# Four real rows as one group of 64-row halves, and planned steps moved behind a section's last tile

## The chip, the cores and the metric

The kernel runs on one core of a Trainium2 chip. The metric is the device time of one execution in microseconds (us). TensorE (PE) multiplies, VectorE (DVE) takes maxima and evacuates, ScalarE (ACT) does exponentials and copies, GpSimd (POOL) does elementwise work, SyncE (SP) issues most DMAs.

## The reference

Two token mixers read the same x (2048 x 512), and a gate per token blends them:

```python
g = sigmoid((x * gate_w).sum(-1))
# A: DFT along the hidden axis, then along the sequence, real part
a = x @ dft_hid_re.T;  b = x @ dft_hid_im.T
A = dft_seq_re @ a - dft_seq_im @ b
# B: attention, 32 heads of 16
q, k, v = split(x @ wqkv)
B = (softmax(q @ k.T * 16**-0.5) @ v) @ wo
out = g * A + (1 - g) * B
```

All arrays are float32. The kernel keeps the accuracy by splitting operands in a high and a low part and adding three products (high with high, high with low, low with high).

## The kernel before

**Units and streams.** Heads go in 16 pairs; head h of a pair (h is 0 or 1) has its stacked q and k in partitions 64h to 64h+49 of the tiles qs and ks (two buffers, by the pair's parity). A *unit* is one pair, one half of the queries (hf, 1024 of them) and one block of 128 keys; there are 512, 32 to a pair. Two kinds of PE tile are made of qs and ks, each 128 x 512 and of 64 rows of PE:

- an *s tile* (scores(), L720) is a block of scores; ACT takes its exponential into pt (L721). There are 2 x 512 for each half h.
- an *a tile* (a_tile(), L222) is a block of scores of which DVE takes the row maxima (L224). The a stream runs 48 a half ahead of the s stream (LEAD); when 64 a tiles of a pair's query half are done, m_parts() and m_rows() put the negated maxima as two extra rows into qs (4 DMAs on SP, 4 on POOL), which the s tiles of that half need.

values() takes two units' pt and does their value products (pv(), L756, 128 rows x 32 columns, four side by side); ACT copies the sum to oe (L765), POOL adds it to osum (L771) in add_sums().

**Sections.** PE's order is written by hand. A tile uses only 64 of PE's 128 rows, so in a *section* (segment()) the products of the Fourier part run in one half of the rows while tiles of the other half's stream run beside them; two sections in a row take the same products in half 0 and then in half 1, into one bank (d_bank, psD), which completes the sum. The strings FULL (16 slots), THIN (14) and NINE give a section's tiles: "s" and "a" have a product beside them, "aS" and "sA" are a tile of each half with no product, and "|" ends it with values(). pairs() yields 13 pairs of THIN sections (12 products, one row block of the real part each), 96 pairs of FULL (16 products of the sequence DFT) and 13 of NINE (9 products of the output projection).

**Ahead of the sections**, four() makes row blocks in groups of four chains: each phase runs two chains side by side, one in each half of the rows, and the halves are swapped in the later phases; after products 3 and 8 of a phase maxima() issues a pair of a tiles. Chain groups of v and of the imaginary part b are made so. The first three row blocks of the real part (real(), L416, then real_next(): ACT copies the bank to y, two buffers, and POOL splits y into the two halves of ab[s]) are done in 128-row products, six at a time (pump()), with four tiles after each six and one values() among them.

**Behind the sections** a loop over the last ten pairs of units issues eight s tiles, some whole products of the projection (table whole) and one values() each, and last_pair() ends the kernel.

**The plan.** at(u, f, ...) notes a step for unit u, and run_plan(u) runs what is noted up to u + 1. Steps are load_stacks() (12 DMAs on SP that load a pair's qs and ks), sums() and inverse() (the softmax sums' reciprocals), block() (normalising a block of outputs: loads on SP, a multiply on POOL, then a cast on ACT, a subtraction on POOL and a DMA), load_yg() and last_block(). deferred holds m_parts and m_rows, of which each section's end runs one.

**Banks.** bank() takes of seven PSUM banks the one that a small model (now, free, dve, act) expects to come free first. Every engine works through its own instructions in the order written.

Of the kernel before, what the change touches and what calls it, by code (L numbers as in the profile page):

```python
# [9 lines left out]
F32 = mybir.dt.float32  # L10
# [5 lines left out]
P = 128  # L16
S = 2048
D = 512
# [4 lines left out]
NT = S // P  # L23
# [8 lines left out]
def mix_kernel(ctx: ExitStack, tc: tile.TileContext, xa_t, xa, wqkv, w_hid, w_seq, wo, gate_w, out):  # L32
# [264 lines left out]
    def maxima():  # L297

        nonlocal a_next
        users = [a_tile(a_next, h) for h in range(2)]  # L300
        a_next += 1
        return users[1]

    def four(ss, wh, wl, done):

        ps = [turn_of("s") for _ in ss]
        seen = None
        for phase, pair in enumerate(((0, 1), (2, 3), (1, 0), (3, 2))):
            guard, seen = seen, None
            both = [row_products(ss[c], wh, wl) for c in pair]  # L310
            for j in range(12):
                for half, c in enumerate(pair):
                    st, mv = next(both[half])
                    r = slice(64 * half, 64 * half + 64)
                    i = nc.tensor.matmul(ps[c], st[r], mv[r], start=phase < 2 and j == 0, stop=phase > 1 and j == 11)  # L315
                    if phase > 1 and j == 0:
                        tc.add_manual_dep(
                            i.ins, guard.ins.name,
                            mybir.DependencyInfo(mybir.DependencyClass.Sync, mybir.DependencyReason.DATA))
                if j in (3, 8):  # L320
                    user = maxima()
                    seen = seen or user
            if deferred:
                deferred.pop(0)()
            if phase > 1:
                for c in sorted(pair):
                    done(ss[c], ps[c])
# [10 lines left out]
    def spare(i, dt, name):  # L338

        return const.tile([P, 4, P], dt, name=name, tag=f"w{i}")  # L340
# [40 lines left out]
    def bank(i=None):  # L381

        nonlocal now
        if i is None:
            i = min(range(7), key=lambda j: free[j])
        now = max(now, free[i] + 0.7)
        return i, banks[i].tile([P, 512], F32, name="t")

    def read_by(i, kind):

        nonlocal dve, act
        if kind == "a":
            dve = max(now + 2.0, dve) + 2.6
            free[i] = dve + 0.4
        else:
            act = max(now + 2.0, act) + 2.1
            free[i] = act + 0.5
# [21 lines left out]

    def real():  # L420

        for s, t in enumerate(ab):
            chain = Chain(d_bank, 12)
            for kt in range(KT):
                h1, l1 = (t[:, v, kt * P:(kt + 1) * P] for v in range(2))
                yield chain, h1, wre[0][kt], None
                yield chain, h1, wre[1][kt], None
                yield chain, l1, wre[0][kt], partial(real_next, s, t, chain) if kt == KT - 1 else None
# [186 lines left out]
    def load_yg(hf, ts):  # L615
        for t in ts:
            if hf:
                yp[t] = spare(t - 8, F32, f"yp{t}").rearrange("p a b -> p (a b)")
            elif t < 3:
                yp[t] = work.tile([P, D], F32, name=f"yp{t}", tag="y" if t else "yr", bufs=2 if t else 1)  # L620
        if not hf and ts[-1] == 7:
            for x, n in (("qs0", 4), ("ks0", 1)):
                y4 = main.tile([P, n, D], F32, name=f"yp_{x}", tag=x)
                yp.update({(3 if n == 4 else 7) + j: y4[:, j] for j in range(n)})
        for t in ts:
            nc.sync.dma_start(yp[t], yg_d[t])

# [76 lines left out]

    pts = {}

    def scores(u, qb, h):
        p, r = divmod(u, 32)
        hf, kt = divmod(r, 16)
        q0 = hf * 1024 + qb * 512  # L710
        if u >= UNITS - 16:

            blk, kt = divmod(kt, 8)
            q0, kt = 1024 + blk * 512, 2 * kt + qb
        if u not in pts:
            pts[u] = work.tile([P, 4, 512], F32, name="pt", bufs=4)
        i, ps = bank()
        read_by(i, "s")
        rr = slice(64 * h, 64 * h + 50)
        nc.tensor.matmul(ps, ks[p % 2][rr, kt * P:(kt + 1) * P], qs[p % 2][rr, q0:q0 + 512], start=True, stop=True)  # L720
        return nc.scalar.activation(pts[u][:, 2 * qb + h], ps, AF.Exp, bias=0.0, scale=DH ** -0.5)  # L721
# [54 lines left out]
    def add_sums():  # L776
        while adds:
            adds.pop(0)()
# [26 lines left out]
    def pump(gen, n):  # L805
        for x in take(gen, n, False):
            issue(x, None)
# [8 lines left out]
    def at(u, f, *args):  # L816
        plan.setdefault(u, []).append(partial(f, *args))
# [10 lines left out]
                        at(last + du + 8 * half, block, step, hf, ct, half)  # L828

    for p in range(1, NP):  # L830
        at(32 * (p - 1), load_stacks, p)
    one, more = [d_bank], [d_bank, o_bank, o_bank]
    at(456, load_yg, 0, range(3))
    at(481, load_yg, 0, range(3, 8))
    for step, u in enumerate((486, 490, 494)):
        at(u, last_block, step, 1, 3, nc.gpsimd)
    for step, u in enumerate((500, 506, 506)):
# [4 lines left out]
    def run_plan(u):  # L842
        for v in sorted(v for v in plan if v <= u + 1):
            for f in plan.pop(v):
                f()
# [31 lines left out]
    def values():  # L877
        nonlocal valued
        us = valued, valued + 1
        valued += 2  # L880
        add_sums()
        if us[0] < UNITS - 16:
            pv(us)
        else:
            for u in us:
                pv_last(u)

    def segment(pattern, half, ds, stop):


        nonlocal now
        nonlocal users
        before, users = users, []
        ds, late = iter(ds), []
        for slot in pattern.split():
            if slot == "|":
                for f in late:
                    f()
                values()
                continue  # L900
            now += 1
            if len(slot) == 1:
                x = next(ds, None)
                if x:

                    before = before if x[0].begun else None
                    i = issue(x, half, stop, late)
                    users = []
                    if before:
                        tc.add_manual_dep(  # L910
                            i.ins, dict(before).get("s", before[0][1]).ins.name,
                            mybir.DependencyInfo(mybir.DependencyClass.Sync, mybir.DependencyReason.DATA))
                        before = None
            score(slot[0], 1 - half)
            if len(slot) == 2:
                score(slot[1].lower(), half)
        if deferred:
            deferred.pop(0)()

    def pairs():  # L920

        for i in range(NT - 3):
            yield (THIN,) * 2, take(hid, 12)
        for i in range(2 * NT * 3):
            yield (FULL,) * 2, take(seq, 16)
        for gen, n in ((proj(1, (0, 1, 2), one), 8), (first, 5)):
            for i in range(n):
                yield NINE, take(gen, 9)

    first = proj(0, (0, 1, 2), one)  # L930
    run_plan(0)
    gate()
    hid, seq = real(), dft()
    for i in range(6):
        pump(hid, 6)
        if i < 4:
            for kind in "sa":
                for h in range(2):
                    score(kind, h)
        else:  # L940
            if i == 4:
                values()
            for _ in range(2):
                score("s", 0)
                score("a", 0)
    users = []
    for patterns, ds in pairs():
        for half in range(2):
            run_plan(valued)
            segment(patterns[half], half, ds, half == 1)  # L950


    run_plan(valued)
    for i in range(4):
        score("s", 1)
    run_deferred()
    assert not any(a_left.values())
    third = proj(1, (3,), more)
    last = proj(0, (3,), more)
    whole = {492: (first, 9), 494: (first, 9), 496: (first, 9), 498: (third, 6), 500: (third, 6), 502: (third, 6),  # L960
             504: (third, 3), 506: (third, 3), 508: (last, 6), 510: (last, 9)}
    for u in range(valued + 2, UNITS, 2):
        add_sums()
        run_plan(u)
        for i in range(4):
            if i == 2:
                pump(*whole[u])
                if u == 506:
                    last_pairs[0].turn()
                elif u == 508:  # L970
                    last_pairs[0].back()
            for h in range(2):
                scores(u + i // 2, i % 2, h)
        if u == 510:
            last_pairs[0].products(())
        values()
    values()
    last_pair(last)

# [35 lines left out]
```

## Time and profile before

| | |
|---|---|
| time, median of 3 (lowest to highest) | 1699.48 us (1699.48 to 1699.53) |
| the profiled execution | 1699.7 us, span 1697.6 us |
| PE busy | 1684.1 us (99%), 13027 matmuls |
| DVE / ACT / POOL busy | 1368.3 (81%) / 1246.5 (73%) / 746.2 us (44%) |
| PE's granted clock | 0.999 of full speed |

How to read the rows quoted below: times are us from the start of the span; a row of the timeline gives start, duration, engine, line of the kernel, operation, output <- inputs, shapes and count, and in brackets the idle time ahead of it and what ended that. A row of the groups ends in total busy us, mean ns of one, and idle time ahead. Matmuls are pipelined: several PE rows overlap, and the distance of two starts says more than a duration. The chain merges a run of instructions into one piece with its start and length.

### The profile page before, as it was taken

The page shows a single profiled execution, that of the slowest core. Times are in us where ns is not written, and L with a number is a line of the kernel's source. Part 1 is how long each engine was busy: PE and PEld are TensorE (multiplying, and loading weights), DVE is VectorE, ACT ScalarE, POOL GpSimd, SP SyncE. Part 2 cuts the span into 40 slices and gives each one's busy share as a digit, 9 for nine tenths or more (in the row PEclk, how much of TensorE's full clock was granted, in tenths as well). Part 3 has the DMA queues.
Part 4 walks back from the last instruction along what each step waited for, and adds up shares of the span by engine and source line. Part 5 has one row for each costly group of instructions (what it writes and reads, how often), then busy time and mean ns, then how long its engine had stood idle before and what let it go on. Part 6 is the DMA issues. An engine that isn't in the chain of part 4 may idle for free.

```text
span 1697.6 us, 34437 instructions
## 1 busy us (share of the span) xinstructions
PE 1684.1 (99%) x13027; PEld 1084.1 (64%) x13027; DVE 1368.3 (81%) x2283; ACT 1246.5 (73%) x2472; POOL 746.2 (44%) x807
## 2 busy tenths in 40 slices
PE   9999999999999999999999999999999999999997
PEld 7888666666666666666666666666666666665543
DVE  5448688888888888888888888888888888899933
ACT  5212388887777777777877778777787778788785
POOL 1114634544444555444544555545455555422230
PEclk9999999999999999999999999999999999999999
DMA  9963602123141525232146535242331534550114
GB/s 300 335 148 118 170 6 37 28 52 64 56 82 40 107 84 104 66 64 52 56 88 239 127 93 109 58 77 63 67 75 54 124 101 94 201 142 7 40 28 137
DMA packets 82485, 165.14 MB, mean 97 GB/s; under 512 B 19776, under 2 KB 20032, under 8 KB 78480
## 3 DMA queue, kind: packets, MB, share of 16 engines
q1 hardware_dynamic: 77968, 162.56, 37.3%
q8 instruction: 102, 1.67, 0.4%
q0 software_dynamic: 4352, 0.39, 0.3%
q14 instruction: 63, 0.52, 0.1%
HBM read 107.73 MB, written 54.52 MB: 96 GB/s over the span
## 4 chain that ended last, share of the span: by engine, by line
PE 98%; DVE 1%; ACT 0%; DMA 0%; POOL 0%; issue 0%; SPq 0%; DVEq 0%; POOLq 0%; ACTq 0%
PE d L416 40%; PE t L756 27%; PE t L222 11%; PE t L720 9%; PE t L315 4%; PE t L88 2%; PE t L89 2%; PE t L90 2%; PE t L333 1%; PE t L737 1%; DVE mx L224 1%; PE t L416 0%; ACT pt L721 0%; PE t L159 0%; DVE yp L597 0%; PE t L675 0%
## 5 line engine op out<-in xcount | busy, mean ns | idle before, releaser
L224 DVE TENSOR_REDUCE mx<-t 128x1 f32<-128x512 f32 x2024 | 1255.3, 684 | 208.8 <-PE t L222 178.9
L721 ACT ACTIVATE pt<-t 128x512 f32<-128x512 f32 x2048 | 1034.6, 633 | 11.0 <-PE t L720 10.8
L720 PE MATMUL t<-qs,ks 50*128 50x512 f32 x2048 | 742.9, 413 | 1.3 <-DVE yp L597 1.2
L222 PE MATMUL t<-ks,qs 48*128 48x512 f32 x2024 | 694.6, 401 | 0.3 <-DVE mx L224 0.2
L416 PE MATMUL d<-xab,ch 64*128 64x512 f32 x2016 | 647.2, 395 | 0.0
L756 PE MATMUL t<-pt,vt 128*32 128x512 f32 x3968 | 478.2, 598 | 0.2 <-ACT pt L721 0.2
L416 PEld LDWEIGHTS d<-xab,ch 64*128 64x128 f32 x2016 | 365.8, 184 | 131.6 <-issue 90.5
L222 PEld LDWEIGHTS t<-ks,qs 48*128 48x128 f32 x2024 | 366.0, 185 | 72.2 <-DVE mx L224 25.3
L416 PE MATMUL d<-xab,cl 64*128 64x512 f32 x1008 | 398.6, 395 | 0.0
L720 PEld LDWEIGHTS t<-qs,ks 50*128 50x128 f32 x2048 | 366.4, 185 | 36.5 <-ACT pt L721 12.7
L771 POOL TENSOR_TENSOR osum<-osum,oe 128x512 f32<-128x512 f32 x217 | 279.1, 1286 | 127.2 <-ACT oe L765 123.4
L765 ACT COPY oe<-t 128x512 f32<-128x512 f32 x217 | 127.3, 587 | 252.8 <-PE t L756 240.6
L756 PEld LDWEIGHTS t<-pt,vt 128*32 128x32 f32 x3968 | 104.9, 109 | 229.5 <-issue 148.7
L371 POOL CAST ch<-craw 128x512 fp32r<-128x512 f32 x126 | 76.8, 610 | 368.3 <-PE t L720 342.2
L416 PEld LDWEIGHTS d<-xab,cl 64*128 64x128 f32 x1008 | 185.6, 184 | 67.5 <-issue 53.6
L372 POOL TENSOR_TENSOR cl<-craw,ch 128x512 fp32r<-128x512 f32 x126 | 162.3, 1288 | 10.1
L416 PE MATMUL d<-wre,xab 64*128 64x512 f32 (+1 forms) x348 | 85.7, 391 | 0.8 <-DVE mx L224 0.7
L245 POOL DMA_DIRECT2D qs<-mt x128 | 71.9, 567 | 27.1 <-DVE mt L241 20.7
L416 PEld LDWEIGHTS d<-wre,xab 64*128 64x128 f32 (+1 forms) x348 | 63.8, 185 | 8.4 <-DVE mx L224 1.1
L416 PE MATMUL d<-wo_hl,o_hl 64*128 64x512 f32 (+1 forms) x261 | 69.2, 392 | 0.0
L416 PEld LDWEIGHTS d<-wo_hl,o_hl 64*128 64x128 f32 (+1 forms) x261 | 47.9, 185 | 4.4 <-issue 0.6
L88 PE MATMUL t<-xab,wh 128*128 128x512 f32 x128 | 50.2, 392 | 0.0
(120 smaller groups left out, 866.3 us busy)
## 6 DMA issues: line engine op xcount, KB each, us to landing
craw<-w_seq SPq DMA_DIRECT2D x128, 256.0 KB
qk<-hl SPq DMA_DIRECT2D x32, 512.0 KB
qs<-qk SPq DMA_DIRECT2D x96, 128.0 KB
ks<-qk SPq DMA_DIRECT2D x96, 128.0 KB
b<-hl SPq DMA_DIRECT2D x16, 512.0 KB
xab<-b SPq DMA_DIRECT2D x16, 512.0 KB
o<-osum SPq DMA_DIRECT2D x62, 128.0 KB
oh<-nh SPq DMA_DIRECT2D x12, 512.0 KB
```

The lines of the kernel that those rows point to most:

```text
L88: nc.tensor.matmul(ps, sh, mh, start=first, stop=False)
L222: nc.tensor.matmul(ps, qs[p % 2][r, qt * P:(qt + 1) * P], ks[p % 2][r, kb * 512:(kb + 1) * 512], start=True, stop=True)
L224: user = nc.vector.tensor_reduce(mx[p % 2][:, h, qt, kb:kb + 1], ps, AX.X, ALU.max)
L245: (nc.sync, nc.gpsimd)[h].dma_start(rows.rearrange("v (q b c) -> v b q c", q=8, b=4)[:, b], mt[hf][32 * b + h:32 * b + 32:2])
L371: nc.gpsimd.tensor_copy(h1, raw)
L372: nc.gpsimd.tensor_tensor(l1, raw, h1.bitcast(F32), ALU.subtract)
L416: i = nc.tensor.matmul(self.ps, st[r], mv[r], start=not self.begun, stop=stop)
L720: nc.tensor.matmul(ps, ks[p % 2][rr, kt * P:(kt + 1) * P], qs[p % 2][rr, q0:q0 + 512], start=True, stop=True)
L721: return nc.scalar.activation(pts[u][:, 2 * qb + h], ps, AF.Exp, bias=0.0, scale=DH ** -0.5)
L756: nc.tensor.matmul(acc[32 * j:32 * j + 32], vt[:, kt, p, h:h + 32], pt[:, j], start=u == us[0], stop=u == us[-1])
L765: nc.scalar.copy(oe, acc)
L771: nc.gpsimd.tensor_tensor(o, o, oe, ALU.add)
```

## The change

- The first *four* row blocks of the real part run as one group of four(), whose new argument between places the first tiles: in each of the four phases one s tile of half 0 and one a tile of half 1 after product 3, and one a tile of each half after product 8 of phases 0 and 2. scores() can be given a bank. bank()'s model starts from seven given times.
- pairs() yields 12 pairs of THIN sections instead of 13; the streams are now three values() behind, so the loop behind the sections runs over 13 pairs of units. It issues the a tiles that are left over and runs the deferred steps, and the 27 projection products that were done nine at a time are done six and three at a time.
- run_plan() runs at a section's end, behind the last tile and add_sums() and ahead of values(), instead of at its start. load_stacks is noted one unit earlier.
- The tile yp[3] gets a buffer of its own and is loaded at unit 456; yp[4] to yp[7] take the buffer of qs[0].

```diff
-    def four(ss, wh, wl, done):
+    def four(ss, wh, wl, done, between=None):
...
                 if j in (3, 8):
-                    user = maxima()
+                    user = between(phase, j) if between else maxima()
                     seen = seen or user
...
     def real():
-        for s, t in enumerate(ab):
+        for s, t in list(enumerate(ab))[4:]:
...
+            elif t == 3:
+                yp[t] = work.tile([P, D], F32, name="yp3")
...
         if not hf and ts[-1] == 7:
-            for x, n in (("qs0", 4), ("ks0", 1)):
-                y4 = main.tile([P, n, D], F32, name=f"yp_{x}", tag=x)
-                yp.update({(3 if n == 4 else 7) + j: y4[:, j] for j in range(n)})
+            y4 = main.tile([P, 4, D], F32, name="yp_qs0", tag="qs0")
+            yp.update({4 + j: y4[:, j] for j in range(4)})
...
-    def scores(u, qb, h):
+    def scores(u, qb, h, ps=None):
...
-        i, ps = bank()
-        read_by(i, "s")
+        if ps is None:
+            i, ps = bank()
+            read_by(i, "s")
...
     for p in range(1, NP):
-        at(32 * (p - 1), load_stacks, p)
+        at(32 * (p - 1) - 1, load_stacks, p)
...
-    at(456, load_yg, 0, range(3))
-    at(481, load_yg, 0, range(3, 8))
+    at(456, load_yg, 0, range(4))
+    at(481, load_yg, 0, range(4, 8))
...
         valued += 2
-        add_sums()
...
             if slot == "|":
                 for f in late:
                     f()
+                add_sums()
+                run_plan(valued)
                 values()
                 continue
...
-        for i in range(NT - 3):
+        for i in range(NT - 4):
             yield (THIN,) * 2, take(hid, 12)
...
+    def first_rows(s, ps):
+        chain = Chain(None, 0)
+        chain.ps = ps
+        real_next(s, ab[s], chain)
+
+    def first_tiles(phase, j):
+        if j == 3:
+            user = scores(*next(streams[0][0]), turn_of("a"))
+            a_tile(*next(streams[1][1]))
+            return user
+        if phase in (0, 2):
+            for h in range(2):
+                a_tile(*next(streams[h][1]))
+
+    four(range(4), *wre, first_rows, first_tiles)
+    free[:] = 0.0, 0.0, 4.0, 4.0, 1.0, 2.0, 3.0
     hid, seq = real(), dft()
-    for i in range(6):
-        pump(hid, 6)
-        if i < 4:
-            for kind in "sa":
-                for h in range(2):
-                    score(kind, h)
-        else:
-            if i == 4:
-                values()
-            for _ in range(2):
-                score("s", 0)
-                score("a", 0)
-    users = []
     for patterns, ds in pairs():
         for half in range(2):
-            run_plan(valued)
             segment(patterns[half], half, ds, half == 1)
...
     for i in range(4):
         score("s", 1)
-    run_deferred()
-    assert not any(a_left.values())
...
-    whole = {492: (first, 9), 494: (first, 9), 496: (first, 9), 498: (third, 6), 500: (third, 6), 502: (third, 6),
-             504: (third, 3), 506: (third, 3), 508: (last, 6), 510: (last, 9)}
+    whole = {486: (first, 6), 488: (first, 3), 490: (first, 6), 492: (first, 3), 494: (first, 6), 496: (first, 3),
+             498: (third, 6), 500: (third, 6), 502: (third, 6), 504: (third, 3), 506: (third, 3),
+             508: (last, 6), 510: (last, 9)}
...
             for h in range(2):
                 scores(u + i // 2, i % 2, h)
+            for h in range(2):
+                score("a", h)
...
         values()
+        if deferred:
+            deferred.pop(0)()
+    assert not any(a_left.values())
     values()
     last_pair(last)
```

## The prediction

> **What bounds the kernel now.** I read the page first, for the shares and the chain of work that ended last:
>
> ```profile
> span 1697.6 us, 34437 instructions
> PE 1684.1 (99%) x13027; PEld 1084.1 (64%) x13027; DVE 1368.3 (81%) x2283; ACT 1246.5 (73%) x2472; POOL 746.2 (44%) x807
> PE 98%; DVE 1%; ACT 0%; DMA 0%; POOL 0%; issue 0%; SPq 0%; DVEq 0%; POOLq 0%; ACTq 0%
> ```
>
> TensorE (PE) carries 98% of the chain, so only what lies in its order, or makes it wait, is worth anything; DVE, ACT and POOL matter where PE waits for them. Then the chain in order of time. Its L756 pieces are the value products that close each section (start, duration), so the distance of two starts is the length of a section:
>
> ```profile
> 215.01 1.85 PE t L756 x16
> ...
> 354.09 1.85 PE t L756 x16
> 359.93 1.85 PE t L756 x16
> ...
> 587.05 1.85 PE t L756 x16
> 593.37 1.85 PE t L756 x16
> 599.18 1.85 PE t L756 x16
> ...
> 1478.54 1.85 PE t L756 x16
> 1483.90 1.85 PE t L756 x16
> 1489.86 1.85 PE t L756 x16
> ...
> 1614.86 1.85 PE t L756 x16
> ...
> 1631.57 1.86 PE t L756 x16
> ...
> 1642.45 1.90 PE t L756 x16
> ```
>
> From 215.01 to 354.09 lie 25 thin sections, 5.56 us each. From 354.09 to 1478.54 lie 192 full sections; 359.93 - 354.09 and 599.18 - 593.37 give 5.82 for a plain one, so 192 would take 1117.4, and they take 1124.45: 7.0 us too many. The NINE sections alternate 5.36 and 5.96, 11.32 a pair. Of the iterations behind the sections the two from 1631.57 to 1642.45 take 5.44 each.
>
> The 7.0 us have an owner. The ACT timeline of a plain section and of the long one before 593.37, PE's weight loads in the latter, and the group of the cast:
>
> ```profile
> 583.22 0.59 ACT L765 COPY oe<-t 128x512 f32<-128x512 f32 x1 [1.34 <-PE t L756]
> 583.70 4.03 ACT L721 ACTIVATE pt<-t 128x512 f32<-128x512 f32 x8
> 589.02 0.59 ACT L765 COPY oe<-t 128x512 f32<-128x512 f32 x1 [1.29 <-PE t L756]
> 589.51 0.62 ACT L84 CAST nh<-no 128x512 fp32r<-128x512 f32 x1
> 590.03 4.02 ACT L721 ACTIVATE pt<-t 128x512 f32<-128x512 f32 x8
> 590.68 0.18 PEld L720 LDWEIGHTS t<-qs,ks 50*128 50x128 f32 x1 [0.16 <-ACT pt L721]
> 592.63 0.18 PEld L222 LDWEIGHTS t<-ks,qs 48*128 48x128 f32 x1 [0.30 <-ACT pt L721]
> L84 ACT CAST nh<-no 128x512 fp32r<-128x512 f32 x12 | 7.5, 624 | 0.0
> ```
>
> In the plain section the eight exponentials start 0.48 behind the start of the copy oe; in the long one a cast nh stands between, they start 1.01 behind it, and from 590.68 to 592.63 PE's tiles wait for ACT to free banks. The section costs 593.37 - 587.05 = 6.32, so 0.50 more. There are 12 such casts: 6.0 of the 7.0 us. Each is issued by the third step of block(), which runs at the start of a section, behind oe and ahead of the exponentials.
>
> **The change, part by part.** The sum is made against the profiled execution, 1699.7 us (span 1697.6); the median, 1699.48, is 0.2 below it.
>
> *The planned steps* now run behind the section's last tile and before the value products. On ACT the cast then stands behind the eight exponentials and ahead of oe. Exponentials that start at 583.70 end at 587.73, the cast would end at 588.35, and the next oe starts at 589.02 because it waits for PE's value products: 0.67 us are free, the cover is those products. Gain 12 x 0.50 = 6.0. Without the cover each cast would delay oe, and with it the next exponentials, by its 0.62. In four of the twelve an activation y of a chain's end stands there too and may use up the free time: so the gain is at least 8 x 0.50 = 4.0; at most it is 7.0, if the other 1.0 us goes as well. I take 6.0, as the rows of one section give it. The other steps issue DMAs on SP, one multiply on POOL, one reciprocal on DVE: behind the last tile they meet DVE and POOL while PE does value products, nothing.
>
> *The first rows.* Before, PE does three chains in 128-row products, six at a time, between tiles:
>
> ```profile
> 188.15 0.40 PE L222 MATMUL t<-ks,qs 48*128 48x512 f32 x2
> 191.41 0.40 PE L222 MATMUL t<-ks,qs 48*128 48x512 f32 x2
> 194.60 1.66 PE L416 MATMUL d<-wre,xab 128*128 128x512 f32 x6 [0.68 <-DVE mx L224]
> 196.19 0.50 PE L720 MATMUL t<-qs,ks 50*128 50x512 f32 x2
> 199.99 0.62 POOL L433 CAST xab<-y 128x512 fp32r<-128x512 f32 x1
> 200.69 1.28 POOL L434 TENSOR_TENSOR xab<-y,xab 128x512 fp32r<-128x512 f32 x1
> 210.82 0.39 PE L222 MATMUL t<-ks,qs 48*128 48x512 f32 x1
> ```
>
> The last four() of the stage before shows the pace of 64-row halves: a phase of 14 slots in 191.41 - 188.15 = 3.26, 0.233 a slot, without a seam. The old group cannot start at the next slot, 193.77, but at 194.60: it waits 0.68 for the maximum that still reads its bank. The new group takes other banks, and starts at 193.77. It has 48 product slots and 6 of tiles (pairs at j = 3 in four phases, at j = 8 in two), 54 x 0.233 = 12.6, end 206.4. The first section starts there, against 210.82 before, where the first value products of a section followed 4.1 later (215.01 less 0.07: the chain stamps value products that much behind their first start, as 1631.57 stands for 1631.50); undisturbed they would come at 210.5, in the chain's stamp 210.6.
>
> But a wait is added. real_next copies four rows to y, which has two buffers. Rows 0 and 1 are complete behind the third phase, 193.77 + 41 x 0.233 = 203.3; ACT has the first by about 204.3, POOL takes 0.62 + 1.28 for each, and row 1's buffer is free at about 208.2. Row 3's copy waits for it until 208.8 (a copy takes 0.59), and queued behind it on ACT are the exponentials of the first section. Its value products need five of them, 0.50 each: 208.8 + 2.5 + 0.4 for ACT's and PE's reaction = 211.7, in the chain's stamp 211.8. That is 3.2 before 215.01. Bounds: 4.4 if PE hides the wait, 1.8 if all eight exponentials must end first.
>
> *Two thin sections less*: 2 x 5.56 = 11.1.
>
> *The end of the sections.* PE's timeline there, and in the iterations behind:
>
> ```profile
> 1623.82 1.92 PE L756 MATMUL t<-pt,vt 128*32 128x512 f32 x14
> 1626.86 1.80 PE L720 MATMUL t<-qs,ks 50*128 50x512 f32 x8
> 1628.59 2.32 PE L416 MATMUL d<-wo_hl,o_hl 128*128 128x512 f32 x9
> 1630.84 0.73 PE L720 MATMUL t<-qs,ks 50*128 50x512 f32 x4
> 1644.90 0.97 PE L416 MATMUL d<-wo_hl,o_lno 128*128 128x512 f32 x3
> 1645.71 0.86 PE L416 MATMUL t<-wo_hl,o_lno 128*128 128x512 f32 x3
> 1646.50 0.73 PE L720 MATMUL t<-qs,ks 50*128 50x512 f32 x3
> ```
>
> Each half has 1024 - 48 = 976 maxima to issue. Before, 122 pairs of sections with 8 each stood behind a start with 8 and 4, so the streams run dry 8 and 4 slots early and the last two sections are shorter. Now 121 pairs follow a start with 2 and 6: the sections stay full, and 6 and 2 maxima are left over. 26 NINE sections at 11.32 a pair are 147.2; before they took 1623.82 + 0.07 - 1478.54 = 145.35. So 1.8 more. The reciprocals of inverse(1, 3) move behind the pairs, and the fifth y tile is loaded one section ahead of its use; if DVE waits for either in front of the last maxima, up to 0.8 on top.
>
> *Three more iterations behind the sections.* Nine products cost 2.25, six 1646.50 - 1644.90 = 1.60, three 0.81. An iteration of 5.44 with six is 4.79, with three 4.00. The first is value products 1.86, then 1.73 + 2.25 + 0.66 from 1626.86 on; with six products 5.85, and the left-over maxima (two pairs, two alone) add 4 x 0.233: 6.78. The second has two more alone, 4.00 + 0.47. So PE alone needs 6.78 + 4.47 + 4.79 + 4.00 + 4.79 + 4.00 = 28.8. ACT, however, needs 4.03 + 0.59 = 4.62 an iteration, so five of them 23.1, and the six 29.9. I take 29.5, near ACT's bound, since PE's 4.79 and 4.00 lie on both sides of 4.62 and the banks let ACT lag a little. From 1623.82 (stamp 1623.89) to 1642.45 the old three took 18.56: 10.9 more; bounds 10.2 (PE alone) and 12.8 (ACT's bound and an exponential's 0.50 more in each of the three added). The last half's bias rows are issued behind the third iteration, two iterations ahead of the scores that read them, some 8.8 us.
>
> The four tiles from 1630.84 to the next value products at 1631.50 take 0.66 where two slots are 0.47, so a change between 128-row, 64-row and value products costs about 0.2; an added iteration has four, a removed section two. The Trainium skill, "TensorEngine Tiling (Array Packing)", Key Properties, speaks against this part: each change of tiling mode drains TensorE. By its "TensorE: Matmul & The Clock Gate", Single matmul latency, an uncovered fill is 398 cycles, an estimate of 0.17 us; the sum would be some 0.4 lower by it, and the rows decide.
>
> **Sum**: -3.2 - 11.1 - 6.0 + 1.8 + 10.9 = -7.6. From the profiled 1699.7 to 1692.1, and 1691.9 against the median. The gains' far ends give -4.4 - 11.1 - 7.0 + 1.8 + 10.2 = -10.5, the others -1.8 - 11.1 - 4.0 + 2.6 + 12.8 = -1.5: 1689.0 to 1698.0.
>
> **Rivals.** *The casts gain nothing* (10%): the oe copy falls behind the cast and hands the delay on, section by section. Against it the 0.67 of free time; for it that the four sections with an activation y show how full ACT's gap can be. Then -1.6, 1697.9, no change that can be told (a measurement here resolves about 0.2%, 3.4 us).
>
> *The stacks come late* (8%), the one on the other side. load_stacks now stands behind a section's tiles, and with the new offsets of the streams one half reads the next pair's stacks from its third tile of the section after the next two:
>
> ```profile
> 471.67 0.42 SPq L209 DMA_DIRECT2D qs<-qk  x1
> 479.16 0.30 SPq L210 DMA_DIRECT2D ks<-qk  x1
> 1650.09 2.14 DMA rc<-o
> ```
>
> The twelve issues take 7.8 us (471.67 to 479.46), landing 2.1, together 9.9. The time is 1.86 + 2 x 5.82 + about 0.7 = 14.2, so 4.3 are spare. If SP's queue is held up for more than 4.3, PE waits at each of 14 pairs; from 0.8 a pair the gain of 7.6 is gone and 3.4 lost: at 1.0 a pair over, 1691.9 + 14 = 1705.9. For it: the twelve issues already take 0.65 each where the first takes 0.42. Against it: they would have to take 1.0 each, and the queue's other DMAs stand at the same distances as before.
>
> **How the numbers follow.** Forecast 82%, of which 2% ends above 1696.1; no gain from the casts 10%; late stacks 8%. So faster by over 0.2% 0.80, within it 0.12, slower 0.08. The range 1689.0 to 1698.0 holds the bounds of the forecast and the second case.
>
> **What would show it.** First value products of a section near 211.8; plain sections still 5.56, 5.82 and 11.32 a pair; no section of 6.32 with a cast nh in it, and nh ahead of oe on ACT; 242 sections' value products end the pairs and six iterations of 6.8, then 4.0 to 4.8, follow. It is wrong if the plain section grows (0.03 over 192 would cost 5.8), if PE waits for qs or ks at pair borders, or if ACT's lag in the tail reaches the DMA chain behind the last value sums.

## The result: 3.3% slower, one term right in kind and wrong in size

The changed kernel takes 1756.78 us (median of 4 runs, 1750.88 to 1759.42) against 1699.51 for the kernel before (1699.48 to 1699.97, 4 runs): ratio 1.0332, 95% interval 1.0305 to 1.0358. Forecast were 1691.9 and 1689.0 to 1698.0. The profiled execution took 1750.88 us; its span of 1749.1 is 51.5 longer than the 1697.6 of before. In the changed kernel the lines have moved by two: value products are L758, scores L722, exponentials L723, the copy oe L767.

The page after, its span, busy row and the chain by engine and by line:

```profile
span 1749.1 us, 34467 instructions
PE 1694.9 (97%) x13063; PEld 1096.3 (63%) x13063; DVE 1372.2 (78%) x2283; ACT 1250.4 (71%) x2472; POOL 746.7 (43%) x807
PE 87%; DMA 9%; SPq 1%; POOL 1%; ACT 1%; issue 1%; DVE 0%; DVEq 0%; POOLq 0%; ACTq 0%
PE d L416 33%; PE t L758 23%; PE t L222 11%; PE t L722 9%; PE t L315 4%; DMA ks<-qk 3%; DMA qs<-qk 3%; PE t L89 2%; PE t L90 2%; PE t L88 2%; DMA craw<-w_seq 1%; PE t L333 1%; PE t L739 1%; ACT pt L723 1%; SPq L210 1%
```

PE had 98% of the chain, now it has 87%, and DMA 9%: the loads of the stacks ks and qs. The waits say who stood still, with total, number and longest in us:

```profile
PEld t L222 <- issue: 41.5, 9, 9.5
PE t L222 <- DMA ks<-qk: 21.3, 4, 9.1
PE t L222 <- DMA craw<-w_seq: 15.6, 5, 5.0
```

All are at L222, the a tile (the first row is its weight loads, for which the profile finds no releaser); in the chain of before DMA had 0%. (The third row names a load of craw, which was issued behind the stacks and is the last on one of the semaphores that the tile waits for; an a tile reads only ks and qs.) Twelve sections carry it all, one at each pair p from 3 to 14, at the third a tile of half 1 in the section of units 32p-28, which is the place that the rival *the stacks come late* names. By the distance of value products they last 8.23, 11.38, 7.04, 12.80, 11.33, 7.25, 9.86, 17.59, 7.29, 10.11, 14.02 and 12.24 us; over twelve plain ones of 5.82 that is 59.3 too many. Without them 1750.88 would be 1691.6.

The longest, at p = 10, on SP's timeline and then on PE's:

```profile
1072.41 0.59 SPq L558 DMA_DIRECT2D oh<-nh  x1
1073.09 0.55 SPq L209 DMA_DIRECT2D qs<-qk  x1
...
1080.76 0.30 SPq L210 DMA_DIRECT2D ks<-qk  x1
```

```profile
1076.92 1.92 PE L758 MATMUL t<-pt,vt 128*32 128x512 f32 x16
...
1080.04 0.39 PE L416 MATMUL d<-xab,ch 64*128 64x512 f32 x1
1089.55 0.76 PE L222 MATMUL t<-ks,qs 48*128 48x512 f32 x1 [9.12 <-DMA ks<-qk]
...
1090.11 0.63 PE L722 MATMUL t<-qs,ks 50*128 50x512 f32 x1
...
1090.54 0.63 PE L722 MATMUL t<-qs,ks 50*128 50x512 f32 x1
...
1094.51 1.92 PE L758 MATMUL t<-pt,vt 128*32 128x512 f32 x16
```

The first of the twelve issues is at 1073.09, the last at 1080.76. The chain in order of time goes through the fourth and the last of them (start, length until it landed):

```profile
1074.97 5.77 DMA ks<-qk
...
1080.76 8.44 DMA ks<-qk
```

The fourth lands at 1080.74, and SP issues the last one right behind it: the issues themselves wait for the transfer. The last lands at 1089.20, which is 16.1 us behind the first issue, and PE starts at 1089.55, 16.5 behind it. The windows show why (length, busy us and count of PE, PEld, DVE, ACT and POOL, granted clock, DMA share, GB/s). First the kernel after, then the kernel before at its own load of the same pair, first issued at 1038.08:

```profile
1073.00:1077.00 4.00, 4.00 (x40) 3.40 (x40) 3.24 (x6) 3.90 (x8) 1.74 (x3) 1.00 0.97 225
1077.00:1081.00 4.00, 3.43 (x27) 1.42 (x27) 3.11 (x5) 2.66 (x6) 2.06 (x2) 1.00 1.03 121
1081.00:1085.00 4.00, 0.00 (x0) 0.00 (x0) 0.00 (x0) 0.04 (x1) 0.00 (x0) 0.90 1.02 121
1085.00:1089.00 4.00, 0.00 (x0) 0.00 (x0) 0.00 (x0) 0.00 (x0) 0.00 (x0) 0.50 0.94 126
1089.00:1093.00 4.00, 3.45 (x16) 3.01 (x18) 2.06 (x4) 1.60 (x3) 0.00 (x0) 0.50 0.35 132
```

```profile
1038.00:1042.00 4.00, 4.00 (x33) 1.77 (x31) 2.67 (x6) 2.70 (x6) 0.60 (x1) 1.00 0.99 229
1042.00:1046.00 4.00, 4.00 (x38) 2.95 (x40) 3.97 (x7) 3.72 (x8) 2.96 (x3) 1.00 1.00 115
1046.00:1050.00 4.00, 4.00 (x39) 2.91 (x29) 3.15 (x6) 3.02 (x7) 0.17 (x1) 1.00 0.98 115
1050.00:1054.00 4.00, 4.00 (x36) 2.04 (x34) 3.17 (x6) 2.66 (x7) 0.31 (x1) 1.00 0.98 123
1054.00:1058.00 4.00, 4.00 (x40) 2.60 (x36) 3.98 (x8) 3.94 (x8) 1.59 (x2) 1.00 0.43 143
```

In both the DMA engines are full for 16 us. By the trace's record of single packets the first 2 us of these belong to the transfer ahead on the queue, oh<-nh; then come the stacks' own 192 packets of 8 KB, for 12.8 us (1075.16 to 1087.92; 12.6 us before). Before, PE is busy through all of it, since nothing needed the stacks sooner; after, it stands still for two whole windows.

### The profile page after: what moved, and what is told of

It is laid out like the page before. It is cut to its first block, busy times and chain, and to the rows that moved or that the text cites. A ratio compares the mean times of both kernels' runs of the same rounds, so it can differ in the third digit from the quotient of the medians.

```text
span 1749.1 us, 34467 instructions
## 1 busy us (share of the span) xinstructions
PE 1694.9 (97%) x13063; PEld 1096.3 (63%) x13063; DVE 1372.2 (78%) x2283; ACT 1250.4 (71%) x2472; POOL 746.7 (43%) x807
## 4 chain that ended last, share of the span: by engine, by line
PE 87%; DMA 9%; SPq 1%; POOL 1%; ACT 1%; issue 1%; DVE 0%; DVEq 0%; POOLq 0%; ACTq 0%
PE d L416 33%; PE t L758 23%; PE t L222 11%; PE t L722 9%; PE t L315 4%; DMA ks<-qk 3%; DMA qs<-qk 3%; PE t L89 2%; PE t L90 2%; PE t L88 2%; DMA craw<-w_seq 1%; PE t L333 1%; PE t L739 1%; ACT pt L723 1%; SPq L210 1%
## 5 line engine op out<-in xcount | busy, mean ns | idle before, releaser
L723 ACT ACTIVATE pt<-t 128x512 f32<-128x512 f32 x2048 | 1038.9, 630 | 67.0 <-PE d L416 48.8
L722 PE MATMUL t<-qs,ks 50*128 50x512 f32 x2048 | 746.6, 417 | 2.5 <-DVE yp L597 1.5
L222 PE MATMUL t<-ks,qs 48*128 48x512 f32 x2021 | 700.8, 405 | 40.7 <-DMA ks<-qk 21.3
L416 PE MATMUL d<-xab,ch 64*128 64x512 f32 x2016 | 656.1, 400 | 0.0
L758 PE MATMUL t<-pt,vt 128*32 128x512 f32 x3968 | 477.1, 598 | 0.0
L416 PEld LDWEIGHTS d<-xab,ch 64*128 64x128 f32 x2016 | 372.9, 187 | 131.7 <-issue 87.2
L222 PEld LDWEIGHTS t<-ks,qs 48*128 48x128 f32 x2021 | 371.6, 188 | 109.5 <-issue 41.5
L416 PE MATMUL d<-xab,cl 64*128 64x512 f32 x1008 | 404.1, 401 | 0.0
L722 PEld LDWEIGHTS t<-qs,ks 50*128 50x128 f32 x2048 | 370.3, 187 | 41.5 <-ACT pt L723 16.5
L767 ACT COPY oe<-t 128x512 f32<-128x512 f32 x217 | 127.7, 588 | 238.1 <-PE t L758 237.0
L758 PEld LDWEIGHTS t<-pt,vt 128*32 128x32 f32 x3968 | 104.8, 109 | 229.1 <-issue 151.3
L416 PE MATMUL d<-wre,xab 64*128 64x512 f32 x288 | 70.3, 389 | 0.0
L416 PEld LDWEIGHTS d<-wre,xab 64*128 64x128 f32 x288 | 52.9, 185 | 4.2
```

Of the source, the lines that this page charges most:

```text
L222: nc.tensor.matmul(ps, qs[p % 2][r, qt * P:(qt + 1) * P], ks[p % 2][r, kb * 512:(kb + 1) * 512], start=True, stop=True)
L416: i = nc.tensor.matmul(self.ps, st[r], mv[r], start=not self.begun, stop=stop)
L758: nc.tensor.matmul(acc[32 * j:32 * j + 32], vt[:, kt, p, h:h + 32], pt[:, j], start=u == us[0], stop=u == us[-1])
L767: nc.scalar.copy(oe, acc)
```

## The experiments

The theory (A): a load of 12 x 128 KB takes about 16 us from its first issue, the changed order of the streams wants it sooner than that, and nothing else is wrong. Rivals: (B) moving the planned steps delays the load, so that the move is to blame; (C) what stands ahead of the load on SP's queue is to blame; (D) the skew of the two halves alone, which the group's first tiles make.

### x1_split: half 1's stacks one section earlier

```diff
-            at(32 * (p - 1) - 1, load_stacks, p)
+            at(32 * (p - 1) - 3, load_stacks, p, (1,))   # half 1
+            at(32 * (p - 1) - 1, load_stacks, p, (0,))   # half 0
```

> The changed kernel, with load_stacks split by half: half 1's six DMAs one section earlier (behind the section of units 32p-36), half 0's where they were. Theory A (a load of 1.57 MB keeps the DMA engines full for some 14.5 us, and the change leaves it too little time before half 1's third tile of the section of units 32p-28): the twelve long sections (59 us in all) go back to 5.82, time 1690 to 1693. Rival B (the moved plan steps disturb the section borders in another way, bias rows or POOL): at least half of the 59 us stays, 1720 or more. Rival C (the DMAs of a chain's end stand ahead of the load on SP's queue): half 1's loads have none ahead of them, so 1690 to 1693 as well.

Measured: 1709.27 (1708.86 to 1709.86), 1.0045 of before (1.003 to 1.006). The waits of pairs 3 to 14 are gone. Two new ones have come, in the section k = 15, 14.56 us long, and in k = 223, 13.52 long (sections are counted by their value products, from 0). They are not a tiles but scores:

```profile
PE t L722 <- DMA ks<-qk: 12.0, 2, 6.0
```

At pairs 2 and 15 the sections are short or the streams offset otherwise, and the early load stands ahead of the last score tiles that still want the pair before last in the same buffer; these tiles wait for it and read the new stacks, so this part is computed otherwise. The theory holds for the twelve waits; the edit was right only for pairs 3 to 14.

### x3_start: the plan back at a section's start

```diff
-            at(32 * (p - 1) - 1, load_stacks, p)
+            at(32 * (p - 1), load_stacks, p)
...
-                run_plan(valued)      # behind the last tile
...
+            run_plan(valued)          # at the section's start
```

> The changed kernel with run_plan back at a section's start and load_stacks at unit 32(p-1), as before the change; first rows, streams and tail as changed. Theory A: on SP's queue the load keeps its place behind the same section, so the waits stay, and the twelve sections with the cast are long again: 1750 to 1765. Rival B (the move of the plan is to blame): no waits, casts back, 1696 to 1699. Rival C: as A.

Measured: 1760.03 (1758.62 to 1760.51), ratio 1.0341 (1.0326 to 1.0357). All twelve waits stay (6.58 to 16.60 us long), and the casts' 6.3 us sections are back, which the waits of PE's weight loads for the exponentials show, 66 here and 16 in the changed kernel:

```profile
PEld t L222 <- ACT pt L723: 21.4, 66, 0.8
```

```profile
PEld t L222 <- ACT pt L723: 10.5, 16, 0.8
```

By the distance of their value products nine sections with a cast are again 6.30 to 6.32 long. So rival B falls.

### x4_move: only the plan moved, in the kernel before

```diff
-        at(32 * (p - 1), load_stacks, p)
+        at(32 * (p - 1) - 1, load_stacks, p)
...
+                add_sums()
+                run_plan(valued)      # behind the last tile
                 values()
```

> The kernel before, with only the planned steps moved behind a section's last tile and load_stacks noted one unit earlier. Theory A: in this order of the streams the load follows a section of half 0, with 20 us and more to its use, so no waits; the twelve casts no longer lengthen their sections: 1693.5, within 1692 to 1695. Rival B: waits as in the changed kernel, 1740 or more. If the casts' gain was not theirs: 1699.5.

Measured: 1693.6 (1692.76 to 1694.63), ratio 0.9951 (0.9934 to 0.9967). No waits at the pairs' borders, no 6.3 us sections; the span is 1691.3, so 6.3 below the 1697.6 of before. The move does what the prediction gave it, 6.0.

### x7_half: half the bytes of each load

```diff
-                nc.sync.dma_start(q_t[part].bitcast(F32), qk_d[0][qv, rows])
+                n = S // 2 if p > 1 else S
+                nc.sync.dma_start(q_t[part, :n].bitcast(F32), qk_d[0][qv, rows, :n])
```

and the same for k: from pair 2 on the second half of the columns keeps older data.

> The changed kernel, with each load of pairs 2 to 15 bringing only the first half of every stack's columns (half of the bytes, as many DMAs, at the same place); the second half keeps old data. Theory A (bytes): the load ends some 7 us sooner, so of the twelve waits (1.2 to 11.8 us) only the longest are left, 1691 to 1699. Rival C (place on the queue) and a fixed time per DMA: the load starts as late and its issues take as long, so most of the waits stay, 1730 to 1755.

Measured: 1695.76 (1694.28 to 1697.14), ratio 0.9966 (0.9953 to 0.9979). The load is issued where the changed kernel issues it, at p = 10 again 7.8 us behind the value products beside which it is planned; eleven of the twelve waits are gone, and p = 10 keeps 1.70 us (PE's timeline; loads issued from 1046.39 on), beside its windows:

```profile
1055.41 0.47 PE L223 MATMUL t<-ks,qs 48*128 48x512 f32 x1 [1.70 <-DMA ks<-qk]
```

```profile
1046.40:1050.40 4.00, 4.00 (x36) 3.20 (x40) 3.35 (x6) 4.00 (x9) 1.71 (x3) 1.00 0.88 222
1050.40:1054.40 4.00, 3.32 (x27) 1.33 (x19) 3.01 (x5) 2.57 (x5) 1.97 (x2) 1.00 0.77 139
1054.40:1058.40 4.00, 2.99 (x25) 2.29 (x29) 2.47 (x4) 2.20 (x5) 0.00 (x0) 1.00 0.55 167
1058.40:1062.40 4.00, 4.00 (x36) 2.37 (x30) 2.89 (x6) 2.66 (x6) 0.43 (x1) 1.00 0.00 0
```

Half the bytes are there after 9.0 us (1055.41 - 1046.39) where all of them take 16.5 to the same tile (1089.55 - 1073.09). The DMAs are as many and stand at the same place of the queue, so the time goes with the bytes, or with the length of the rows, which is halved too; the issuing shrinks along with it, from 7.7 to 5.6 us (1046.39 to 1051.98). That is the theory's main point, and neither C nor D gives it.

### x2_order: the load ahead of the other steps on SP

```diff
-        at(32 * (p - 1) - 1, load_stacks, p)
+        (plan if p == 1 else loads)[32 * (p - 1) - 1] = [partial(load_stacks, p)]
...
+                run_plan(valued, loads)     # as soon as the last tile is issued
                 ...
                 run_plan(valued)
```

> The changed kernel, with load_stacks run ahead of the steps of a chain's end (a store of y or yr, a craw load) instead of behind them, so that the loads stand in front of these on SP's queue; nothing else moved. Rival C (the queue order alone makes the loads late): the twelve waits, 59 us, vanish, 1691 to 1695. Theory A with the order as a part: only the four pairs whose load stands behind a chain's end (4, 7, 10, 13; 5.6, 5.5, 11.8 and 8.2 us) come down to the 1.2 to 1.5 of pairs 5, 8 and 11; the other eight keep theirs: about 25 saved, 1725 to 1732. Order of no weight: 1750 or more.

Measured: 1714.24 (1709.64 to 1724.62), ratio 1.0088 (1.0057 to 1.0119): between A's and C's numbers. The load now starts 0.8 before to 1.3 behind the value products, where the changed kernel has 0.4 to 7.8 behind them, and the longest wait of p = 10 shrinks to:

```profile
1071.99 0.47 PE L222 MATMUL t<-ks,qs 48*128 48x512 f32 x1 [1.18 <-DMA ks<-qk]
```

Its section is 7.42 us instead of 17.59, and the twelve are 5.96 to 10.89 long. So rival C is a part: what stands ahead of the load on SP's queue (in the rows above oh<-nh, which starts only at 1072.41) sets how long the longest waits are, and about 42 of the 57 us go with it (1756.78 - 1714.24). But with that gone the load is still late: eleven of the twelve sections are 0.7 us and more too long. (The lengths are those of the profiled run, 1724.62, the longest of the four.)

### x6_skew: first maxima four and four

```diff
-        if phase in (0, 2):
-            for h in range(2):
-                a_tile(*next(streams[h][1]))
+        a_tile(*next(streams[0][1]))
```

> The changed kernel, with the first group's maxima dealt 4 and 4 instead of 2 and 6 (four single a tiles of half 0 in place of two pairs, so two slots more there, and two less behind the sections). Half 1 then reads a new pair's stacks from its fifth a tile, not its third, four slots of 0.23 us later. Theory A: each of the twelve waits is about 0.9 us shorter, 11 saved, 1738 to 1748. If the distance from load to use is not what counts: 1750 to 1760.

Measured: 1741.06 (1736.06 to 1743.7), ratio 1.0234 (1.0215 to 1.0253). Half 1's first maxima go from six to four, so it wants the new stacks two of its a tiles later; the long sections stay (6.06 to 15.79 us). Half 1 then starts with the four of the kernel before, and 16 of the 57 us go (1756.78 - 1741.06). So the skew, rival D, is a part too, because it sets how soon the stacks are wanted, and not the cause by itself.

### x5_late: the load later in the kernel before

```diff
-        at(32 * (p - 1), load_stacks, p)
+        at(32 * (p - 1) + (2 if p > 1 else 0), load_stacks, p)
```

> The kernel before with one thing changed: for pairs 2 to 15 the stacks' load is issued at the start of the section of units 32(p-1)+2 and no longer of units 32(p-1); nothing else of the change is in it. Theory A (the load comes too late for the first tile of the new pair, and nothing else of the change matters): one section of 5.8 us later, the load begins about a microsecond after the value products of the section at which it began 4.8 us before them, which is where the changed kernel has it at its cheapest pairs; half 1 of this kernel wants its first new tile about a section later than in the changed kernel, so the waits are 0 to 3 us at most of the 14 borders: 1699 to 1735 us, with the waits at the borders k = 16p-13 or one to either side, and the casts' 6.3 us sections still there. Theory B (the changed kernel's waits come of its half-row group and its order, whatever the load's place): 1699.5 us and no section above 6.5.

Measured: 1777.77 (1773.83 to 1788.07), ratio 1.0476 (1.0442 to 1.051). The theory's kind of wait comes into the kernel before by a later load alone, at 13 of 14 borders (pairs 2 to 14), but more of it than the 1735 that I allowed. Pair 9's queue on SP and PE's wait:

```profile
993.72 1.12 SPq L774 DMA_DIRECT2D o<-osum  x2
994.88 1.30 SPq L456 DMA_DIRECT2D yr<-yr  x1
996.28 0.37 SPq L209 DMA_DIRECT2D qs<-qk  x1
```

```profile
1011.95 0.76 PE L222 MATMUL t<-ks,qs 48*128 48x512 f32 x1 [7.99 <-DMA ks<-qk]
```

From the first issue to the tile it is 15.7 us, again. What I missed is the issue: I had put it a microsecond behind the value products, and it was 2.4 to 8.4 behind them, since other DMAs stand ahead of it at this section too.

### x1b_split and x9_wait: a version without the waits

x1b_split splits the load as x1_split does, for pairs 3 to 14 only. x9_wait is x1b_split with buffers of their own for the copies y of rows 2 and 3:

```diff
-        y = work.tile([P, D], F32, name="y", bufs=2)
+        if s in (2, 3):
+            y = work.tile([P, 2, D], F32, name="yf", tag=("no", "nh")[s - 2])[:, 0]
+        else:
+            y = work.tile([P, D], F32, name="y", bufs=2)
```

> As x1_split, but pairs 2 and 15, whose half 1 is still being read in THIN and NINE sections when the earlier loads would come, load both halves where the changed kernel does. x1_split had left two waits, 9.0 us at pair 2 and 7.6 at pair 15, and none in the full sections. Theory A: no wait at any pair, 1709.3 - 16.6 = 1692.7, within 1691.5 and 1693.5. If the two waits were of another kind: 1700 or more.

> x1b_split, with two further buffers for the copies y of the first group's rows 2 and 3, so that row 3's copy waits for no split on POOL. By the prediction's step (the copy's wait delays the first section by 1.2 us against an undisturbed one): first value products at about 210.5 instead of 211.6, and the time 1 us below x1b_split's. If PE hides the wait: the same time as x1b_split.

Measured: x1b_split 1691.98 (1691.86 to 1694.99), ratio 0.9952 (0.994 to 0.9964), with no wait at any pair; x9_wait 1691.49 (1691.15 to 1692.12), ratio 0.9947 (0.9933 to 0.996). Both beat the kernel before, by about 0.5%. Between the two, 0.5 us, the intervals can't tell; the profile can, in ACT's timeline, the changed kernel first:

```profile
206.20 0.59 ACT L432 COPY y<-t 128x512 f32<-128x512 f32 x1 [1.32 <-PE t L315]
207.75 0.59 ACT L432 COPY y<-t 128x512 f32<-128x512 f32 x1 [0.96 <-POOL xab L434]
208.23 4.03 ACT L723 ACTIVATE pt<-t 128x512 f32<-128x512 f32 x8
```

```profile
206.21 1.08 ACT L435 COPY yf<-t 128x512 f32<-128x512 f32 x2 [1.32 <-PE t L315]
207.17 4.04 ACT L726 ACTIVATE pt<-t 128x512 f32<-128x512 f32 x8
```

Row 3's copy no longer waits 0.96 for POOL, and the exponentials start 1.06 earlier.

## Why the prediction was wrong

**The step that failed** is the price in the rival *the stacks come late*: "The twelve issues take 7.8 us ..., landing 2.1, together 9.9. The time is ... 14.2, so 4.3 are spare." Its place and its mechanism were right, and it stood at 8%. The load takes 16.5 us to the tile where 9.9 were counted, and it starts late. In its parts:

- *The landing.* The 2.14 came from a DMA of rc, 12 to 16 KB at the kernel's end; a DMA of the stacks brings 128 KB, and eleven more come with it. No row of the kernel before gives the stacks' own landing, since nothing waited for it, but the DMA share of its windows above stays at 0.98 to 1.00 from 1038 to 1054, and that was there to be read. A sign stood in the prediction's own row, too: issues that take 0.65 each where the first takes 0.42 were waiting for the transfer. At p = 10 the last issue took 8.44 to land.

- *The time available* was 15.0 and not 14.2: the third a tile is the sixth slot of its section, 3.35 behind the start of the value products (1080.27, the slot that stayed empty, less 1076.92), where 1.86 + 0.7 was counted. From the first issue to the tile the load takes 15.4 to 16.5 at the twelve pairs. This alone turns 4.3 spare into 0.4 to 1.5 short, at every one of them.

- *The issue.* I counted from the value products beside which the load is planned. It is issued in order on SP, and starts 0.4 to 7.8 us behind them, 2.5 in the mean of the twelve. At p = 10, 16.5 + 7.8 - 15.0 gives a wait of 9.3; the row says 9.12. The prediction named what would decide ("If SP's queue is held up for more than 4.3") and then held against it that the queue's other DMAs stand at the same distances; before, the load of pair 10 too starts behind an oh<-nh, but it had a section more of time.

- *The clock.* The wait costs more than its length: the windows give 0.50 of full speed from 1085 to 1093, and the tiles after the wait follow each other at 0.43 (1090.11 to 1090.54, the next score) where 0.23 is usual. From 1089.55 to the value products it takes 4.96 where 2.47 were left (a plain section's 1076.92 + 5.82 less 1080.27), so 2.5 us are added to this wait. The Trainium skill's "TensorE: Matmul & The Clock Gate", Part 1: The HAM clock gate, has the clock go to half after an idle window of about 3.4 us; the trace agrees, with 9.1 idle and 0.50. But less was enough here: waits of 2.15 and 2.41 us (p = 9 and 12) were followed by 0.50 as well, for some 3.4 us each from 985.2 and 1282.2 on, and their sections are 4.0 and 4.3 us too long; behind a wait of 1.97 (p = 3) the clock stayed at 1.00, while in x2_order 1.79 and 1.91 (p = 14 and 9) were enough, so the length of the wait alone doesn't decide.

The twelve waits cost 59.3 where the rival priced 14 at 1.0 each. What was left out of the chances is that 4.3 us of slack stood on a row of another transfer: with the load's own length the rival was the likeliest case.

**The other steps**, each against its measure. With the 59.3 of the twelve sections taken out the span is 7.8 shorter than before, where the sum had 7.6, and x1b_split, which only takes the waits away, gives 1691.98 against 1691.9. That is closer than the terms are, and in part luck: one is 0.7 too low, and the others are 0.2 to 0.4 off the other way.

*The casts*, -6.0: no 6.32 section is left. The cast stands ahead of oe, and the next exponentials are not late:

```profile
603.74 2.11 ACT L723 ACTIVATE pt<-t 128x512 f32<-128x512 f32 x4
605.71 0.64 ACT L84 CAST nh<-no 128x512 fp32r<-128x512 f32 x1
607.10 0.59 ACT L767 COPY oe<-t 128x512 f32<-128x512 f32 x1 [0.75 <-PE t L758]
607.58 4.06 ACT L723 ACTIVATE pt<-t 128x512 f32<-128x512 f32 x8
```

The copy oe still finds 0.75 of idle ahead of it, as the 0.67 free said. x4_move gives 6.3 for it. The rival *the casts gain nothing* falls.

*The first rows*, -3.2, value products forecast at a start of 211.7:

```profile
208.39 0.50 PE L722 MATMUL t<-qs,ks 50*128 50x512 f32 x1 [0.93 <-ACT y L432]
...
211.34 1.92 PE L758 MATMUL t<-pt,vt 128*32 128x512 f32 x16
```

So -3.6, and the wait for row 3's copy is there, for 0.93. x9_wait, where it isn't, has them at 210.29; the forecast for that bound was 210.5.

*Two thin sections*, -11.1: from the second on the thin sections take 5.52 to 5.58, so right by their length.

*The end of the sections*, +1.8, and *three more iterations*, +10.9 (six in 29.5), by the value products that begin them, PE's timeline at three places:

```profile
1516.79 1.50 PE L758 MATMUL t<-pt,vt 128*32 128x512 f32 x12
...
1663.73 1.92 PE L758 MATMUL t<-pt,vt 128*32 128x512 f32 x16
...
1693.87 1.50 PE L758 MATMUL t<-pt,vt 128*32 128x512 f32 x12
```

The 26 NINE sections take 146.94 (forecast 147.2), 1.6 more than the 145.35 of before. The six iterations take 30.14, +11.6 and not +10.9, within the bounds. The last five are ACT's, as the step had it: from 1674.11 on no row of ACT has idle time ahead,

```profile
1678.18 0.59 ACT L767 COPY oe<-t 128x512 f32<-128x512 f32 x1
...
1696.16 0.68 ACT L767 COPY oe<-t 128x512 f32<-128x512 f32 x1
```

and these two are four iterations apart, 4.50 each where I counted 4.62. The excess is the first iteration, 7.85 instead of 6.78 (1663.73 to 1671.58): I took it by PE alone, at 0.23 a tile, but from 1666.44 to 1668.85 the tiles come some 0.5 apart: PE's weight loads wait there for banks, 0.31 and 0.32 for ACT's exponentials, and 0.22 and 0.33 for DVE's maxima.

In the step on changes of tiling mode, twelve are added and four removed, so at the 0.17 named there in place of 0.2 the sum would be some 0.3 lower, not 0.4; no run here separates such a change.

Added up: -3.6 for the first rows, -17.4 for casts and thin sections together, +1.6, +11.6 and +59.3 are 51.5, the difference of the spans.

**Not settled**: why the stacks' packets are slow. At p = 10 each packet of 8 KB holds its engine for 1.07 us (median), in x7_half each of 4 KB for 0.35, so less than half. Each of these DMAs writes 16 partitions, and the same bytes in another shape were not tried.

## What to carry to other kernels

A transfer's price is read from its own rows: from first issue to last landing, at its own size and with its own queue full. A row of another transfer isn't a bound, and a hidden load shows its true length only in the DMA share of the windows. When a change makes a consumer come earlier, ask for each double-buffered load whether first issue plus that length still lies ahead of the new first reader, at every period and not at one, since what stands ahead on an in-order queue differs from period to period. And where only one half of a load is wanted early, splitting the load keeps the change's gain: here 1692.0 instead of 1756.8.

## What the chip showed that I had not expected

Twelve DMAs of 128 KB, each to 16 partitions, fill all 16 DMA engines for 12.8 us at some 121 GB/s by the windows' last column, where the window that holds most of the transfer ahead of them shows 225; with half the bytes in each the packets are through in 5.4 us (1048.35 to 1053.76). A PE wait of 9.1 us is followed by 0.50 of the clock up to the end of its section and cost 11.8 us in all, and waits of some 2 us already brought the clock to 0.50.
